# Interleaved two-layer memory attention with gated FFNs: one head grouping for all steps, weight pieces to match, kept tokens of fill blocks, one pool of FFN weight tiles, and a new stored order

## The chip, the cores and the metric

The kernel runs on one core of a Trainium2 chip. The metric is the device time of one execution in microseconds (us); the median of three runs of the kernel before is 1747.63 us. The engines are named as in the profile: PE (matrix products; PEld is its weight load, which overlaps), DVE, ACT and POOL (element work; POOL also issues transfers), and SP, which only issues transfers. Each engine works through its own instructions in the order in which they were issued, and waits for another engine or a transfer only through semaphores.

## The reference, cut to what matters

The input x has 2048 tokens of width D = 512. Two layers are computed, each a recurrent attention and then a gated feed-forward network (FFN), both with a LayerNorm ahead of them and a residual around them; both layers use the same weights.

```python
for s in range(64):                       # 64 segments of 32 tokens, one after another
    h = concat([mem, x[32*s : 32*s+32]])  # 8 memory tokens + 32 tokens = 40
    q, k, v = h @ Wq, h @ Wk, h @ Wv      # 32 heads of 128
    p = softmax(mask(q @ k.T * scale))    # 40 x 40 for each head
    o = sum over heads of (p @ v) @ Wo    # 40 x 512
    mem, out[s] = o[:8], o[8:]            # memory for the next segment
x = x + out;  x = x + (sigmoid(n(x) @ w_gate) * (n(x) @ w_up)) @ w_down   # F = 1792, n: LayerNorm
```

The memory makes the 64 segments of a layer a chain: the Q and K of a segment need the output of the one before.

## The kernel before

**Steps.** The program has 70 steps (`NSTEPS`, L384). Layer 2 follows layer 1 by six segments (`lag`), so steps 6 to 63 treat a segment of each layer together, with 2 x 40 = 80 columns, and steps 0 to 5 and 64 to 69 one segment of one layer, with 40 columns. In steps 0 to 5 the Q and K product carries 14 more columns of layer 2's later segment (54 in all), which are kept in `kx`/`xq` and fetched in steps 6 to 11 (66 columns then).

**One step** (`emit_step`, L771). The heads come in groups. For each group: Q and K by weight tiles of 128x128 (L868), a copy to `qku` by ACT, scores (L904), mask and softmax on DVE and ACT into `pb`, transposes of the probabilities on PE (L950), copies of the transposed blocks into `ptsb` on ACT or DVE (the "spread", L952 to L962: the first as it is, the further ones scaled by a column of zeros and ones, so that the blocks form a block-diagonal matrix), the product with V (L976), a copy to `otsb`, and the sum over heads with `Wo` (L995), whose end releases the next step.

**Head units.** Several heads are stacked on the partitions, one below another, 40 rows each, so that one product with V treats them together; such a stack is a unit. Two-layer steps use `self.sets[3]`: 11 units of three heads (the last of two), taken two units, that is six heads, at a time (6 groups, `self.groups[3]`). One-layer steps use `self.sets[2]`: 16 units of two heads, three units (six heads) at a time, also 6 groups (the last one unit). The probabilities lie in a tile of 66 or 80 columns for each unit, so a one-layer step has 16 transposes of 66 columns and 16 products with V of 2 x 40 = 80 columns.

**V.** V of the tokens is computed ahead, in blocks of four segments (`v_pass` L621ff with matmuls at L635, `v_half` at L673), copied to a staging tile, stored to DRAM (`scr`), and read into the step's `vsb` tile, laid out as the units need; the V of the memory and of the next few tokens comes in the step itself from a strip (matmuls at L762, staging tile `sst`). Because the two groupings lay V out differently in the same tile, `vlast` keeps the last readers of the other layout (L810, L841).

**Start.** `load_weights` (L506) puts the 16.8 MB of attention weights on SP's queue (the loading line is L511): `wv` in 8 pieces of four heads, with x blocks between; then `wq` and `wk` in pieces of 3 + 3, 7 + 7 and 6 + 6 heads, and `wo` in 12 pieces. PE meanwhile computes V of many blocks. The FFN weights (L1089, L1090, L1114) are loaded anew for each of the 32 FFNs, 256 KB at a time, by POOL's queue, into three rings of three tiles (`wg`, `wu`, `wd`); the same nine tiles are staging space for V during the start (`bootp`).

**LayerNorm.** `layernorm_T` normalises 128 tokens and transposes them with four PE products of 128 columns (L595). `pre1` (L735) does it for each block of layer 1. Five blocks (6, 9, 12, 14, 15) are treated twice: once early in `v_fill` (L745), through `ln_x` (L727), which fills free columns of V products with some of their tokens, and later in `pre1`.

**Order.** The program is first listed as tasks with their dependences; a stored permutation (`SEQUENCE`) gives the order of all of them and the choice of engine where a task may go to ACT or DVE, or to the queue of SP or POOL. `replay` (L268) then gives out the places in the pools, and `warm` (L332) picks places where dummy products of a constant tile `hot` (L1214, "fillers" below, 128 to 512 columns each) go ahead of a PE task.

Of the kernel before, what the change touches and what calls it, by code (L numbers as in the profile page):

```python
# [12 lines left out]
BF16 = mybir.dt.bfloat16  # L13
F32 = mybir.dt.float32
# [39 lines left out]
;BKuib6o%lfB&)8j78VFm3*TORJaEeTpTegcj@45cPG=tDu9Cop`gL7BsLuS#OcT}UGbOE%Rvw4_#4%#$D8H!O&97}fvKE=gc~;{D3dThKHFPlwO_o2ZQj%uAntT#b%`=yVSW>zYu00~2SQlskfdun`!ZJ6nE#G~2&?9uc>M  # L54
LJNnK-{6`f<-+4RJ5CZd)}8nOvSmvfKo;s^%eOTt@Z&QQEIDAOJ$@LXy<?hJ}y#Zz34w>^3(tr#O*O)I|-p(v0&hCE6Z=I!u---baa4+5Qm3gUS*53l_a{9Qz2=DO#NG?#SMBs;mj8X%L0%-jPDBKdp!x5<|&*NtR7P%o}ua
+-XmYACJ&^@_Q*%Pqd)VfD(Os7%#QMrvJwasc?e7tW4e|DX`7=(P4&9b1jfW|}nyY`GtB?m|%9YiB{%_E6Z!fQiku2zXKR#fd!bVX{cdYYw6Oa38sdpui0&m(%kDO5RoywpWe0S&Odat#pJd*Y7&%qi}11M_2zTDH){}yQ57
CfOg{V(1Y$JmfqyIFwi1i0YD(h(Op*uWQ$hJP;Bf$yQikUbL75}K_CCXhEehY;YAKq*!3Uc%Xg9$$6Whfxhc_;!XnaeXsWETb0$)eOXEs9v^~2GKd~)jxtdFb@D02?xh_1fp?KW&fTj7T(bbip<45F%z<Q6F`V0&|>^`^b?P
qJ8zT^ZMn>Wcly5FU_gC4bg<ct_t?VIQ91i<1%2up=CHX$olDJee`BwTFh$S(4b<7J|(ro=5g4z*Oc`7TsdGat-Gu458Br)V!dZ#th}Vr^2k08taR4-icZnRx1)Jh)>hE~oGsr}+TM9h@FLc<(r!wd_Q)l$@#>Gc$q3H~Iu8
B@vGI?!$xWWOMXWIIV?oY_(Nj>~oPrOXhF>kb>ie>V?Z|=S{vC&%nc&mvj8fqJ`ng-1GxzLO~&l^?UGKdDeu&>V<rn<D;V-Yi3I0U}(d~*VL}SKef_{vihFam*0lE<Q@4Z?!Z?qE-e`<gdP%rljFd}%1N*?wM}ezvJGP{k@D
$cH#i)?<HymwHhj3y7oDOxbMj(>d6(b!Q+d{(|M_LSlswhN@?|yLvdUV@!>Nk$<yx}-KsEGBSCDfS=C0>x5r{0(p(QEni`j5ECChA3J3+en0nRK&Hcp0NU*(n0!X;LFq2XQO*by|ReBHqg1wB7#*M>TgpbMjBrkTU*99uz+V  # L60
k!4**({(MLwZLEUo#F;deCBV;>LUumfbyI^#!VVbWP5k$-hsK6I{?fV507ZWSJA|AKq%5F`{1CT0QO{)ll|TX=i|DlMvH>_RLPExPwr>G%@9qVJCKh;rJ^&U%*#K4T$Bg>MQlaj#5~$wQ1)H`pM<6emLUsv5wZa)l=){WY>u
1(PrWo8E^2D1I#8XB}8^Ls58~C54o1mj9OA=J+4cPJ+C~sE6k-4&k&ae8X@1F*PsyyFKxb}E<#az2vB}bAQfMX9~5e*e$-cp^b9f#?03PK`_`n347*v6d*kvVd(fEI<GLWdxm4xgBjG)zHL<A%hHEU$OjEB|ok8=Cu$=eft9
7_JwIX$h#wrX%4N>63C6uPVrKBqwjc=Vd@Wy~8jdNx%!(V^~Ph9_85K>}$3*W3jY72M%q-H4DV^R-6iEOJ<_onUb;)O1COU`_I=L_mgyEsJnxeRz8#POUxE1#+`%tEHD44RMPKPW^6eLOcg$o|&zDQ*Nlh>iGK+Ghz|0@nBH
3@kJ$7L<PbAV5AQh4``a`I0#dHH`LBDjM_gK0Pokn)8B2ttp<26cW=A>zgZ=GO3UYclYMQ4dn2>GShncV~(3@lyHdJ{Jxa}Ev3bHmy8Ju@Y9U5ZOE{tO3BJ?jMkiXS|(HfS}kpQC!uhJ!P;9O?}a}e4k*3%iLJX}sgs?w*f=
XgOYGH+cDIV@@a$5ATCuWU#jzExY(5)4aL591Nl?Cx*&6;_u8b|t1>vv?9?^2O-VCaBfCOdyxTq$9dd#ckGW`ET=Jsl6ax*&>JZ_FFIw!m8X)CrH>W%g(JF;g<^At9hhyT|Qp?Z|jy+Uer{4w&$jkIBgR53c-sRQow3V#L`(
$vOBv=vhmUZm13`YMUteDoxBd1P0m9LI(WM5`uXI&1aAxTFXju&Ji(eQ^U~REWO_?68u>zskkLyO|6tP<C+xDQOlw7+iIh5@LT8^X=f)(22(!Me;J5V!ELHErSKTQXZXR{g{GJy12S<ZzfCN&_f+>u8DO|Jvk>@w@&Hj344s
I|6$C3w)^Rgo%Th{vHyA@A7o%+MiYqR?NYb*Y5Cl7XF4+4jP*A>w1`7uq!uTw4y()O)#;`oa-qa=opjk&K5e9gSYBSz3O@(Ud9tbkDP4Tt_3rrXNO|B`^d17v$?eRRhHbXfZ&b=Hgm#DK{Z*>#!yD*yWgOC2CYqRvybr9GP>
# [300 lines left out]
class Kern:  # L368
    def __init__(self, ctx, tc, x_in, mem0, Wq, Wk, Wv, Wo, w_gate, w_up, w_down, out, lag=6, ring=8):
# [17 lines left out]
        self.HH = H // 2  # L387
# [906 lines left out]
```

## Time and profile before

| what | value |
|---|---|
| three runs | 1746.31, 1747.63, 1748.25 us |
| profiled execution, span from first to last instruction | 1747.1 us |
| PE busy | 1733.4 us, 39162 matmuls |
| PEld, DVE, ACT, POOL busy | 85%, 71%, 65%, 49% of the span |
| data moved | 273.41 MB, 156 GB/s on average |
| instructions | 91842 |

The profile gives no time of the profiled execution apart from its span; the median of the runs is 0.5 us above that span. A line of the profile names the engine, the line of the program, the operation, its output and inputs, how many there were, the busy time and the mean duration in ns, and at its end the idle time ahead of them with what ended it. Matmuls overlap: the mean duration of one is not the spacing from one to the next, which is what a row of several products shows by its start and the next row's start.

### The profile page before, as it was taken

What the parts mean: (1) busy time and instruction counts of PE and PEld (TensorE: products, weight loads), DVE (VectorE), ACT (ScalarE), POOL (GpSimd) and SP (SyncE); (2) the same over time, 40 slices, a digit from 0 to 9 for tenths busy, and PEclk for the clock granted to TensorE, in tenths of its full rate; (3) what the DMA queues carried; (4) which work ended last, traced back from release to release, by engine and by line L of the source; (5) the groups of instructions that cost most, each with busy time, mean ns of one, the idle gap of its engine ahead of it and who ended that gap; (6) DMA issues with size and microseconds to landing.
All of it is one profiled execution on the core that took longest, in us unless ns stands there. A gap on an engine that the chain in (4) does not pass through costs nothing.

```text
span 1747.1 us, 91842 instructions
## 1 busy us (share of the span) xinstructions
PE 1733.4 (99%) x39162; PEld 1491.8 (85%) x39162; DVE 1248.4 (71%) x4208; ACT 1128.5 (65%) x3119; POOL 859.0 (49%) x1367
## 2 busy tenths in 40 slices
PE   9999999999999999999999999999999999999998
PEld 4688789889898988989888888989888888988886
DVE  5677777677767776786777767776777776767676
ACT  3576777566666766666666666666665666666564
POOL 5624345635544554445445554544455364454543
PEclk9999999999999999999999999999999999999999
DMA  8935355645645555545555464545455464554644
GB/s 285 320 100 155 109 151 161 195 113 153 174 130 163 156 159 143 165 125 164 152 148 158 136 184 128 166 138 153 132 174 166 139 174 128 144 156 131 178 120 134
DMA packets 145583, 273.41 MB, mean 156 GB/s; under 512 B 39686, under 2 KB 86018, under 8 KB 145174
## 3 DMA queue, kind: packets, MB, share of 16 engines
q0 software_dynamic: 72944, 198.79, 39.8%
q1 hardware_dynamic: 72230, 68.75, 13.3%
q8 instruction: 307, 5.03, 1.2%
q14 instruction: 102, 0.84, 0.2%
HBM read 221.78 MB, written 27.07 MB: 142 GB/s over the span
## 4 chain that ended last, share of the span: by engine, by line
PE 94%; DMA 3%; DVE 1%; SPq 1%; issue 1%; POOL 0%; ACT 0%; POOLq 0%; ACTq 0%
PE bank L868 34%; PE bank L995 17%; PE bank L1097 12%; PE bank L762 8%; PE bank L635 6%; PE bank L1120 6%; PE bank L904 4%; PE bank L976 4%; PE bank L950 2%; PE bank L595 1%; PE bank L1214 1%; DMA wk_sb<-in_A_Wk_dram 1%; DMA wo_sb<-in_A_Wo_dram 0%; PE bank L1065 0%; DMA scr<-wu 0%
## 5 line engine op out<-in xcount | busy, mean ns | idle before, releaser
L868 PE MATMUL bank<-hT,wq_sb 128*128 128x80 bf16 (+3 forms) x8960 | 616.4, 198 | 1.0 <-DVE hT L1008 0.3
L868 PE MATMUL bank<-hT,wk_sb 128*128 128x80 bf16 (+3 forms) x8960 | 616.3, 198 | 0.8 <-DMA wk_sb<-in_A_Wk_dram 0.6
L1228 ACT CAST qku<-bank 128x480 bf16<-128x480 f32 (+4 forms) x770 | 384.7, 508 | 223.7 <-PE bank L868 194.6
L868 PEld LDWEIGHTS <-wq_sb 128*128 128x128 bf16 x8960 | 454.2, 99 | 32.1 <-issue 15.1
L868 PEld LDWEIGHTS <-wk_sb 128*128 128x128 bf16 x8960 | 446.9, 99 | 1.1 <-DMA wk_sb<-in_A_Wk_dram 0.7
L995 PE MATMUL bank<-otsb,wo_sb 128*128 128x80 bf16 (+1 forms) x8960 | 360.2, 198 | 2.2 <-DMA wo_sb<-in_A_Wo_dram 1.3
L918 DVE TENSOR_TENSOR st<-bank,cst 40x240 f32<-40x240 f32 (+3 forms) x768 | 280.5, 368 | 113.2 <-PE bank L904 97.5
L995 PEld LDWEIGHTS <-wo_sb 128*128 128x128 bf16 x8960 | 336.6, 99 | 15.5 <-DMA wo_sb<-in_A_Wo_dram 2.0
L1228 ACT CAST otsb<-bank 128x480 bf16<-128x480 f32 (+3 forms) x420 | 200.2, 483 | 83.4 <-PE bank L976 52.8
L1090 POOL DMA_DIRECT2D wu<-in_B_w_up_dram x217 | 166.5, 768 | 170.0 <-PE bank L950 36.4
L1114 POOL DMA_DIRECT2D wd<-in_B_w_down_dram x217 | 156.9, 723 | 182.0 <-PE bank L1120 39.6
L1224 POOL DMA_DIRECT2D vsb<-sst x351 | 178.2, 512 | 129.6 <-ACT sst L1228 64.7
L1089 POOL DMA_DIRECT2D wg<-in_B_w_gate_dram x217 | 166.4, 767 | 138.1 <-PE bank L1097 56.7
L928 ACT ACTIVATE st<-st 80x240 f32<-80x240 f32 (+3 forms) x420 | 159.2, 381 | 58.0 <-DVE st L925 54.8
L1097 PE MATMUL bank<-xnT,wg 128*128 128x128 bf16 (+2 forms) x1784 | 171.5, 218 | 0.0
L1097 PE MATMUL bank<-xnT,wu 128*128 128x128 bf16 (+2 forms) x1784 | 171.1, 218 | 0.0
L930 DVE TENSOR_REDUCE small<-st 80x6 f32<-80x240 f32 (+3 forms) x420 | 151.5, 363 | 23.4 <-ACT st L928 20.2
L1220 ACT ACTIVATE ptsb<-bank,small 120x160 bf16<-120x160 bf16 (+3 forms) x430 | 156.6, 386 | 17.2 <-PE bank L950 10.7
L904 PE MATMUL bank<-qku 128*128 128x80 bf16 (+1 forms) x2240 | 162.7, 197 | 1.0 <-issue 0.9
L925 DVE TENSOR_TENSOR st<-st,small 80x240 f32<-80x240 f32 (+3 forms) x420 | 155.0, 370 | 5.7
L939 DVE TENSOR_TENSOR pb<-st,small 80x240 bf16<-80x240 f32 (+3 forms) x420 | 154.1, 370 | 5.7
L923 DVE TENSOR_REDUCE small<-st 80x6 f32<-80x240 f32 (+3 forms) x420 | 152.5, 364 | 6.2
(108 smaller groups left out, 2554.1 us busy)
## 6 DMA issues: line engine op xcount, KB each, us to landing
wg<-in_B_w_gate_dram POOLq DMA_DIRECT2D x220, 256.0 KB, 4.2
wu<-in_B_w_up_dram POOLq DMA_DIRECT2D x220, 256.0 KB, 4.2
wd<-in_B_w_down_dram POOLq DMA_DIRECT2D x220, 256.0 KB, 3.9
vsb<-scr SPq DMA_DIRECT2D x137, 66.0 KB
scr<-vst SPq DMA_DIRECT2D x90, 96.0 KB
vsb<-scr POOLq DMA_DIRECT2D x93, 66.0 KB, 3.4
vsb<-sst SPq DMA_DIRECT2D x179, 32.0 KB
vsb<-sst POOLq DMA_DIRECT2D x169, 32.0 KB, 2.8
```

What stands on the lines that cost most here:

```text
L868: nc.tensor.matmul(o_ap, lhsT=W[:, c, h * P:(h + 1) * P], rhs=mv(c), start=(c == 0), stop=(c == DC - 1))
L904: nc.tensor.matmul(s_all(SB)[:, w0 + i, :], lhsT=fview(qku[:, i, 0, 0:1], [(1, P)]), rhs=qku[:, i, 1, 0:ncol], start=True, stop=True)
L918: pl.add("DVE", dve_ns(n, True), lambda gsz=gsz, hs=hs, st=st, SB=SB, pj_=pj_, npj_=npj_, mk=mk, idx=idx: nc.vector.tensor_tensor(out=st[p ...
L928: pl.add("ACT", act_ns(n), lambda hs=hs, st=st: nc.scalar.activation(out=st[pr, hs], in_=st[pr, hs], func=ACTF.Exp, scale=self.scale), r=s ...
L995: nc.tensor.matmul(WB[:, c * ncol:(c + 1) * ncol], lhsT=self.wo[:, h, c * P:(c + 1) * P], rhs=otsb[:, hl, 0:ncol], start=(h == 0 and c == ...
L1089: pl.add("POOL", 760, lambda wg=wg, fs=fs: nc.gpsimd.dma_start(out=wg[:], in_=self.wgv[:, :, fs]), r=[("wo", self.H - 1)], w=[gk] + bt, la ...
L1090: pl.add("POOL", 760, lambda wu=wu, fs=fs: nc.gpsimd.dma_start(out=wu[:], in_=self.wuv[:, :, fs]), r=[("wo", self.H - 1)], w=[uk] + bt, la ...
L1097: nc.tensor.matmul(gu[:, 2 * i + k, 0:n], lhsT=W[:, c, i * P:(i + 1) * P], rhs=xnT[:, c, rw], start=(c == 0), stop=(c == DC - 1))
L1114: pl.add("POOL", 760, lambda wd=wd, ip=ip: nc.gpsimd.dma_start(out=wd[:], in_=self.wdv[:, 2 * ip:2 * ip + 2, :]), w=[dk] + (["boot"] if se ...
L1220: nc.scalar.activation(out=dst, in_=src, func=ACTF.Copy, scale=by)
L1224: {"SP": nc.sync, "POOL": nc.gpsimd}[tk.on].dma_start(out=got[1], in_=got[2])
L1228: nc.scalar.copy(out=dst, in_=src)
```

## The change

- One grouping, `self.rows` and `self.groups`, serves all steps: three heads per unit and two units per group in the one-layer steps too. The V loads of these steps are cut to match (3 instead of 6 from `scr`; 6 instead of 4 from the strip), and `vlast` is gone, since there is one layout.
- The weight pieces follow the units: `wq`, `wk` and `wo` in three rounds, of 3 pieces of three heads, 3 pieces of five, and one piece of eight.
- In `ln_x`, the transposed normalised tokens of the five fill blocks are copied to a staging tile and stored to DRAM (`xt`); `pre1` reads them back (`kept_x`) in place of a second LayerNorm.
- The three rings become one pool of nine tiles (`wtp`), from which each FFN weight and the staging of the start take a tile; a helper `weight` issues the loads.
- The bank pool loses its limits for two kinds of tasks (`{"bg": 3, "v": 3}`), which `replay` only asserts.
- A new stored permutation is used (not shown).

```diff
-        self.sets = {2: [list(range(self.HH)), list(range(self.HH, H))],
-                     3: [list(range(8 * i, 8 * i + 8)) + list(range(24 + 3 * i, min(27 + 3 * i, H))) for i in range(3)]}
+        self.rows = [list(range(8 * i, 8 * i + 8)) + list(range(24 + 3 * i, min(27 + 3 * i, H))) for i in range(3)]
...
+        self.groups = []
+        for u in range(0, self.NU, 2):
+            us = list(range(u, min(u + 2, self.NU)))
+            self.groups.append(([r[k] for k in us for r in self.rows if k < len(r)], us))
...
+        self.xt = dr.tile([self.NBLK * P, D], BF16, name="xt")
...
-        self.wg = [c.tile([P, DC, 2 * P], BF16, name=f"wg{i}") for i in range(self.NG)]
-        self.wu = [c.tile([P, DC, 2 * P], BF16, name=f"wu{i}") for i in range(self.NG)]
-        self.wd = [c.tile([P, 2, D], BF16, name=f"wd{i}") for i in range(self.ND)]
+        self.wt = [c.tile([P, 1024], BF16, name=f"wt{i}") for i in range(9)]
...
-        parts = {0: 3, 3: 6, 9: 7}
-        for heads, us in self.groups[2]:
-            n = len(us)
+        for us in (range(0, 3), range(3, 8), range(8, 11)):
+            hs = [(8 * i + us[0], len(us)) for i in range(3)] if us[0] < 8 else [(24, 8)]
             for nm, sb, v in (("wq", self.wq, wq_v), ("wk", self.wk, wk_v)):
-                for h0 in (us[0], self.HH + us[0]):
-                    m = parts.get(us[0])
-                    if m:
-                        cs = slice(h0 * P, (h0 + m) * P)
-                        ld(sb[:, :, cs], v[:, :, cs], P * self.DC * m * P * 2, [(nm, h) for h in range(h0, h0 + m)])
-            for h0 in (us[0], self.HH + us[0]):
+                for h0, n in hs:
+                    cs = slice(h0 * P, (h0 + n) * P)
+                    ld(sb[:, :, cs], v[:, :, cs], P * self.DC * n * P * 2, [(nm, h) for h in range(h0, h0 + n)])
+            for h0, n in hs:
                 ld(self.wo[:, h0:h0 + n, :], wo_v[:, h0:h0 + n, :], P * n * self.D * 2, [("wo", h) for h in range(h0, h0 + n)])
...
+        pst, B = self.layernorm_T(xb[:, :], key)
+        nc, pl, D = self.nc, self.pl, self.D
+        tt = pl.buf(self.vstp)
+        pl.add(("ACT", "DVE"), copy_ns(D, True), lambda: (tt[:, 0:D].rearrange("p (c n) -> p c n", c=self.DC), pst()), r=[B], w=[tt])
+        pl.add(("SP", "POOL"), {"SP": 430, "POOL": 590}, lambda: ("dma", self.xt[b * P:(b + 1) * P, :], tt[:, 0:D]), r=[tt], w=[("xt", b)], lat=3000.0, nb=P * D * 2)
+        self.kept.add(b)
+        return pst, B
+
+    def kept_x(self, b):
+
+        nc, pl, D = self.nc, self.pl, self.D
+        tt = pl.buf(self.xnp)
+        pl.add("SP", 430, lambda: nc.sync.dma_start(out=tt[:, :], in_=self.xt[b * P:(b + 1) * P, :]), r=[("xt", b)], w=[tt], lat=3500.0, nb=P * D * 2)
+        return (lambda: tt[:, :].rearrange("p (c n) -> p c n", c=self.DC)), tt
...
-        pst, B = self.layernorm_T(xb[:], ("xs", i))
+        pst, B = self.kept_x(b) if b in self.kept else self.layernorm_T(xb[:], ("xs", i))
...
-        ni = 3 if both else 2
-        rows, groups = self.sets[ni], self.groups[ni]
+        rows, groups = self.rows, self.groups
...
-            return vt[r, j, c:c + m] if both else fview(vt[r, 0, 0:1], [(1, 2 * self.NU * P)])[:, c:c + m]
+            return vt[r, j, c:c + m]
...
-            if not both:
-                pcs = [(L * i, h0 - r[0] + o // P, hh) for i, r in enumerate(rows) for h0 in (r[0], r[8]) for o, _, hh in self.runs(h0, 8)]
...
-            hu, hi_ = (1, nu) if ni == 2 else (3, 1)
+            hu, hi_ = 3, 1
...
+                wg, wu = gk, uk = pl.buf(self.wtp), pl.buf(self.wtp)
+                for wt, nm in ((wg, "wg"), (wu, "wu")):
+                    self.weight(wt, nm, jp, [wt], [("wo", self.H - 1)])
...
+                wd = dk = pl.buf(self.wtp)
+                self.weight(wd, "wd", ip, [wd], [("wo", self.H - 1)])
```

More of the change, by code (lines that the diff above doesn't have):

```diff
@@ L145 @@
+qzI#W6;{xHslkB&LfZf
 """
@@ L467, in setup_tiles @@
         self.sstp = Pool(self.sst)
-        self.bootp = Pool([fview(w[:, 0, 0:1], [(1, 1024)]) for w in self.wd + self.wg + self.wu])
+        self.wtp = Pool(self.wt)
         self.xnp = Pool(self.xn)
```

269 lines of the change are left out of this document (118 added, 151 removed).

## The prediction, made before the changed kernel had run

> **What bounds the kernel now.** I read the page first: busy shares, the 40 slices, and the chain of work that ended last.
>
> ```profile
> PE 1733.4 (99%) x39162; PEld 1491.8 (85%) x39162; DVE 1248.4 (71%) x4208; ACT 1128.5 (65%) x3119; POOL 859.0 (49%) x1367
> ...
> PE   9999999999999999999999999999999999999998
> ...
> PE 94%; DMA 3%; DVE 1%; SPq 1%; issue 1%; POOL 0%; ACT 0%; POOLq 0%; ACTq 0%
> ```
>
> PE is busy 99% of the span and is 94% of the chain; the others have slack. So an edit is worth what it takes from PE's instruction stream, or from PE's waits. To see where waits are, I asked for busy times by stretch: up to the first V product (10.23 us), to the end of step 0, of step 5, of step 63, of step 68, and the rest.
>
> ```profile
> 0.00:10.23 10.23, 9.17 (x36) 3.72 (x37) 4.22 (x13) 1.76 (x2) 3.65 (x19) 1.00 0.70 214
> 10.23:79.65 69.42, 64.97 (x783) 36.02 (x783) 41.27 (x121) 32.55 (x87) 42.59 (x85) 1.00 0.96 325
> 79.65:167.10 87.45, 87.21 (x2581) 74.67 (x2580) 65.91 (x235) 65.32 (x243) 36.30 (x58) 1.00 0.49 139
> 167.10:1618.90 1451.80, 1450.10 (x32305) 1273.82 (x32306) 1048.53 (x3533) 956.75 (x2546) 718.58 (x1120) 1.00 0.53 150
> 1618.90:1710.60 91.70, 90.59 (x2708) 79.58 (x2705) 67.28 (x239) 57.83 (x192) 45.30 (x68) 1.00 0.53 152
> 1710.60:1747.10 36.50, 31.36 (x756) 23.96 (x754) 21.23 (x70) 14.25 (x49) 12.57 (x18) 1.00 0.44 126
> ```
>
> Columns: stretch, length, then busy us of PE, PEld, DVE, ACT, POOL, then granted clock, DMA share, GB/s. In one-layer steps (rows 3 and 5) and two-layer steps (row 4) PE lacks 0.2, 1.1 and 1.7 us: bound by PE's stream. The second row differs: PE lacks 4.45 us while DMA is at 96% and 325 GB/s. There the landing of the weights sets the end, as the end of step 0 shows on PE's timeline (a bracket is the idle time ahead and what ended it):
>
> ```profile
> 77.49 0.47 PE L995 MATMUL bank<-otsb,wo_sb 128*128 128x40 bf16 x12 [0.49 <-DMA wo_sb<-in_A_Wo_dram]
> 78.58 0.84 PE L995 MATMUL bank<-otsb,wo_sb 128*128 128x40 bf16 x20 [0.62 <-DMA wo_sb<-in_A_Wo_dram]
> 79.26 0.48 PE L1214 MATMUL bank<-hot 128*128 128x512 bf16 x2
> 79.70 0.26 PE L868 MATMUL bank<-hT,wq_sb 128*128 128x54 bf16 x4
> ```
>
> The last `wo` piece releases the last 20 products; then comes step 1. From 79.70 on, PE runs solid.
>
> **Prices.** Durations of single matmuls overlap, so I take spacings, start to start, from the timeline of a one-layer step and, for wider products, from two pieces of the chain.
>
> ```profile
> 106.29 0.25 PE L950 MATMUL bank<-cst,pb 66*128 66x66 bf16 x3
> 106.38 0.23 PE L904 MATMUL bank<-qku 128*128 128x40 bf16 x3
> ...
> 107.87 0.38 PE L976 MATMUL bank<-ptsb,vsb 80*128 80x80 bf16 x6
> 108.08 1.03 PE L635 MATMUL bank<-wv_sb,xvf 128*128 128x512 bf16 x4
> ```
> ```profile
> 118.05 1.81 PE bank L868 x72
> 520.71 1.79 PE bank L1097 x32
> ```
>
> 66 columns: (106.38 - 106.29)/3 = 30 ns; 80 columns: 0.21/6 = 35 ns; 54 columns: 1.81/72 = 25 ns; 128 columns: 1.79/32 = 56 ns; 512 columns: four from 105.35 to 106.21, 215 ns.
>
> **The change, part by part.** I compared the built instruction lists of both programs, engine by engine, in order.
>
> *Three heads per unit.* A one-layer step has 11 instead of 16 transposes: 192 of 66 columns become 132, -60 x 30 ns = **-1.8 us**, on PE. The products with V go from 16 of 80 columns to 10 of 120 and one of 80 in each step; the columns barely differ: 120 columns take 52 ns (a row of four at L976 in a two-layer step starts at 301.12, the next at 301.33), so 16 x 35 = 560 ns become 10 x 52 + 35 = 555 ns: **-0.1 us** in 12 steps. The price is on ACT and DVE: five groups in each of 12 steps have three spreads instead of two (60 more).
>
> ```profile
> L1220 ACT ACTIVATE ptsb<-bank,small 80x120 bf16<-80x120 bf16 x24 | 8.6, 358 | 1.5 <-PE bank L950 1.1 <-DVE ptsb L1230 0.3
> L1228 ACT COPY ptsb<-bank 40x120 bf16<-40x120 bf16 x21 | 5.1, 248 | 0.1
> ```
>
> Before: 248 + 358 = 606 ns. After, by the rows of two-layer steps (80 columns: 218 plain, 324 scaled): 218 + 2 x 324 = 866 ns, +0.26 us per group, 30 groups x 0.26 x 2 = 15.6 us of ACT or DVE time, of which both have a quarter free in those stretches (65.32 and 65.91 of 87.45 busy). What hides it: between a group's transposes and its V product lie other groups' Q, K and V products, at least 0.6 us of them in both programs, so two spreads on one engine do not quite fit and some V products may wait. Bounds: 0 (all hidden) to +3 us (a fifth of the 15.6 uncovered); I take **+0.5**, close to the hidden end, since PE lacks only 0.24 us in steps 1 to 5 with these spreads in the same place. The loads to `vsb` (3 instead of 6, 6 instead of 4) are on SP and POOL, half idle; nothing.
>
> *Kept tokens.* Five LayerNorms with four transposes each go: -20 x 56 ns = **-1.1 us** on PE. Their DVE and POOL work was off the path (71% and 49%). Added: five copies of 512 columns (0.6 us on ACT), five stores and five loads of 128 KB, on queues with DMA at 53%; their readers are tokens of a block that starts four segments later: nothing. If the load were late, the step's Q and K would wait; I see nothing queued so tightly.
>
> *One pool of weight tiles.* The same 256 KB loads, with any free tile instead of the next of a ring. PE's work between a load's issue and its use, summed by the prices above over the built order, is at least 5.9 us after, 6.5 before (one case 4.8), against landings of 4.2, 4.2 and 3.9 us on the page. Nothing, with a rival below.
>
> *Weight pieces and the start.* Ahead of the last `wo` piece, SP carries 20.24 MB instead of 20.01: 0.23 MB / 325 GB/s = **+0.7 us**, if landing still ends step 0. Fillers: 28 ahead of the first V product become 20 (512 columns mostly, 5.9 to 4.1 us), and between it and the end of step 0, none become 22 (4.4 us at 0.2 each). The latter stand where weights are awaited; if they are, they are free. Q and K can start after nine heads instead of six: 3 x 2 x 0.131 MB = 0.79 MB, +2.4 us, made good if the end is the last `wo` anyway. Bounds for the start: -4 (V 1.8 us sooner, and a 2.1 us wait for `wv` near 20 us closed) to +6.8 (4.4 + 2.4); taken: +0.7, since the row of `wo` at 78.58 is nearest.
>
> *Order.* Between the last `wo` products of a step and the first Q of the next, steps 0 to 2 had nothing; now step 0 has 0.86 us of other work to cover the copy of the memory (the wait at 79.3, filled by two fillers, 0.44 us): **-0.4**. In the two-layer steps the covers (medians) are the same: 0.
>
> Sum: 1747.1 - 1.8 - 0.1 + 0.5 - 1.1 + 0.7 - 0.4 = 1744.9 us of span; +0.5 to the median of the runs (1747.63 - 1747.1): **1745.4 us**.
>
> The granted clock is 1.00 in every stretch, and no idle time in the trace exceeds 2.1 us. The Trainium skill ("TensorE: Matmul & The Clock Gate", "Part 1: The HAM clock gate") says that about 3.4 us of idleness halve the clock, and some 3.4 us of work restore it; no run shown here reaches that. By that rule a start that waited longer, unfilled, would lose another 1.7 us (3.4 us of work at half rate), an estimate from that page; it speaks for the new fillers. The same page ("Back-to-back issue gap") gives about 81 ns for each 128-column product in a stream of weight loads and products; by it the 20 LayerNorm transposes would be worth 1.6 us and the time 1744.9. The trace has 56 ns, and decides.
>
> **Rivals.**
> A, the forecast: PE's stream shrinks by 3 us, the start ends with the last `wo`. 1745.4, by the bounds of the spread 1743 to 1748.
> B: the start shortens. First V products 1.8 us sooner, and the wait for `wv` closed: 1745.4 - 0.7 - 1.8 - 2.1 = 1740.8. For it: PE has idle time there. Against: DMA is at 96%, so PE sooner does not end sooner.
> C, slower: step 0 waits for nine heads of `wq` and `wk`, and fillers run where nothing is missing: 1745.4 - 0.7 + 2.4 + 4.4 = 1751.5. It decides when the fillers stand after the landing of what they precede. Against: the same bytes end the step.
> D, slower: loads of FFN weights with 0.6 us less lead make PE wait 0.2 us in each of 32 FFNs: +6.4, 1751.8. It decides when landings exceed 5.9 us; the row has 4.2.
> E: the 66-column and LayerNorm work removed was itself a cover, and waits take its place: 1747.6, no change.
>
> **How the numbers follow.** Chances: A 0.46, B 0.30, C 0.10, D 0.07, E 0.07. What a measurement can tell from no change is 0.2%, 3.5 us: faster is below 1744.1, slower above 1751.1. Of A, 0.10 lies below 1744.1. Faster: 0.30 + 0.10 = 0.40; same: 0.36 + 0.07 and 0.01 of C = 0.44; slower 0.16. The range reaches to B's 1740.8 with 1 us below, and to the edge of C and D: 1739.8 to 1751.6.
>
> **What would show it.** Right: 132 transposes of 66 columns at the same spacing, 300 LayerNorm transposes, PE in the one-layer steps still within 0.5 us of full, the end of step 0 ended by `wo`, a granted clock of 1.00. Wrong: a bracket on the V product (L976's successor) naming ACT or DVE; PE waits on `wg`, `wu`, `wd`; a first Q product with a long `wk` wait; or two-layer steps whose stretch differs by over 2 us, which nothing above foresees.

## The result, and the profile after

The changed kernel takes **1759.91 us** (median of 6 runs, 1757.88 to 1763.96) beside 1747.94 us of the kernel before on the same chip (6 runs, 1746.16 to 1754.47): ratio 1.0065, 95% interval 1.0049 to 1.0082. It is slower by 12 us where 2 us less were predicted, and outside the range. The profiled execution has a span of 1757.3 us, 10.2 us more than the one of before.

The page of the changed kernel, the lines that answer to the first fence of the prediction:

```profile
PE 1724.7 (98%) x38832; PEld 1490.2 (85%) x39035; DVE 1258.4 (72%) x4149; ACT 1153.6 (66%) x3223; POOL 867.0 (49%) x1390
...
PE   8899999999999999999999999999999999999998
...
PE 89%; DVE 4%; DMA 3%; issue 2%; ACT 1%; POOL 0%; SPq 0%; DVEq 0%; POOLq 0%; ACTq 0%
```

PE was busy for less (1724.7 for 1733.4 us; 203 of its 39035 products, PEld's count, have no record) in a longer span, its first two slices are at 8, and its share of the chain fell from 94% to 89%. The same busy times by stretch (up to the first V product, end of step 0, of step 5, of step 63, of step 68, and the rest):

```profile
0.00:8.00 8.00, 6.39 (x28) 2.58 (x29) 4.71 (x17) 2.14 (x3) 5.54 (x26) 1.00 0.66 203
8.00:85.99 77.99, 69.05 (x791) 37.94 (x800) 40.08 (x113) 36.56 (x102) 42.62 (x81) 1.00 0.95 311
85.99:174.45 88.46, 87.45 (x2521) 74.41 (x2528) 67.23 (x240) 67.28 (x260) 36.48 (x58) 1.00 0.51 141
174.45:1629.61 1455.16, 1440.21 (x32107) 1272.87 (x32283) 1057.35 (x3477) 971.03 (x2587) 724.84 (x1139) 1.00 0.53 151
1629.61:1721.87 92.26, 91.10 (x2652) 79.18 (x2660) 69.17 (x238) 61.21 (x216) 45.95 (x70) 1.00 0.50 141
1721.87:1757.30 35.43, 30.52 (x741) 23.22 (x739) 19.83 (x68) 15.37 (x55) 11.57 (x17) 1.00 0.38 114
```

"Busy" hides most of what happened: a matmul of some 200 ns that starts every 25 ns leaves no hole in the sum of busy times when a start is late. So I counted the matmuls of both programs and gave each its spacing, by the prediction's rows (columns x 0.417 ns + 2.3 ns, at least 25 ns: 25, 30, 35, 56, 216 ns for 54, 66, 80, 128, 512 columns). Length less work less fillers is PE's idle time. In us:

| stretch | length before, after | work | fillers | idle |
|---|---|---|---|---|
| to the end of step 0 | 79.45, 85.99 | 62.52, 62.58 | 5.88, 8.47 | 11.06, 14.94 |
| steps 1 to 5 | 87.47, 88.47 | 82.90, 81.87 | 0.97, 1.08 | 3.60, 5.50 |
| steps 6 to 63 | 1451.80, 1455.16 | 1418.32, 1417.63 | 2.92, 2.43 | 30.57, 35.09 |
| steps 64 to 68 | 91.70, 92.26 | 87.20, 86.39 | 0.32, 0.97 | 4.18, 4.89 |
| the rest | 36.72, 35.42 | 27.89, 27.30 | 1.08, 0.54 | 7.74, 7.58 |

Two things blur the first rows. The end of step 0 is set 0.2 us behind the start of its last `wo` product before, and 0.5 us behind it after; from last `wo` product to last `wo` product the start is 6.2 us longer and steps 1 to 5 are 1.4 us longer. And the first fillers start 427 ns apart instead of 216, up to 6.5 us before and 3.8 us after (the trace's record of the clock begins there, so the first stretch reads 1.00): 2.7 and 1.2 us of the idle in the first row are this slow running.

The work is 3.0 us less, as predicted. The start takes 6.5 us more, the two-layer steps 3.4 us, and the one-layer steps 1.6 us more instead of 1.8 us less. Profiles of one kernel differ by some us in the start, so I also use the kernels of this study that leave a stretch alone: the start took 76.6 to 80.5 us in seven profiles with the start of before (some with other spreads in step 0) and 84.1 to 86.0 in three with the changed one (90.3 in a fourth, a_dve, whose clock was halved for 6.8 us); steps 6 to 63 took 1451.5 to 1454.3 in eight profiles in the order of before and 1455.2 to 1457.1 in seven in the changed order (1456.7 and 1458.9 in two more, whose clock was halved for 3.4 us there). Both gaps are real; in steps 1 to 5 (87.5 to 89.3, and 88.5 to 90.6) the ranges overlap.

PE's timeline at the end of step 0 of the changed kernel, which answers to the prediction's fence from that place:

```profile
73.20 1.08 PE L1198 MATMUL bank<-hot 128*128 128x512 bf16 x5
76.46 0.47 PE L963 MATMUL bank<-ptsb,vsb 120*128 120x120 bf16 x6 [2.17 <-DMA vsb<-sst]
...
84.08 1.57 PE L981 MATMUL bank<-otsb,wo_sb 128*128 128x40 bf16 x56
85.71 0.81 PE L620 MATMUL bank<-wv_sb,xvf 128*128 128x512 bf16 x3
86.36 0.27 PE L855 MATMUL bank<-hT,wq_sb 128*128 128x54 bf16 x4
```

No `wo` product (L981) waits any more. The first V product of step 0 does (L963), after five fillers; it starts at 76.46 us, where before it started at 67.58. What PE waited for in the whole execution, largest first (us in total, times, longest):

```profile
PE bank L620 <- DMA wv_sb<-in_A_Wv_dram: 3.7, 3, 1.5
PE bank L963 <- DMA vsb<-scr: 3.0, 2, 1.9
PE bank L963 <- DMA vsb<-sst: 2.2, 1, 2.2
PE bank L855 <- DMA wk_sb<-in_A_Wk_dram: 1.4, 1, 1.4
```

The loads of V into `vsb` are new in this list, and nothing waits for the FFN weights in `wt`: rival D did not come. Where the V loads stand in SP's queue explains the first of them. Before (SP's timeline: two of the V loads, then the last `wo` pieces; three of the other loads from `scr` for step 0 go between 41 and 51 us and a small one at 60 us, on SP's and POOL's queues):

```profile
46.29 2.58 SPq L1224 DMA_DIRECT2D vsb<-scr  x1
49.33 1.78 SPq L1224 DMA_DIRECT2D vsb<-scr  x1
...
60.20 0.45 SPq L511 DMA_DIRECT2D wo_sb<-in_A_Wo_dram  x1
62.03 0.63 SPq L1224 DMA_DIRECT2D scr<-wu  x1
62.71 9.38 SPq L511 DMA_DIRECT2D wo_sb<-in_A_Wo_dram  x10
```

After, the same queue:

```profile
60.11 4.25 SPq L499 DMA_DIRECT2D wo_sb<-in_A_Wo_dram  x3
64.40 1.84 SPq L1208 DMA_DIRECT2D vsb<-scr  x1
66.29 0.70 SPq L499 DMA_DIRECT2D wo_sb<-in_A_Wo_dram  x1
67.42 0.89 SPq L1208 DMA_DIRECT2D vsb<-scr  x2
68.36 0.40 SPq L499 DMA_DIRECT2D wo_sb<-in_A_Wo_dram  x1
68.87 0.93 SPq L1208 DMA_DIRECT2D vsb<-sst  x1
```

The program ties them together: a V load of step 0 may go only after the `wo` piece that holds the last head (`+ ([("wo", self.H - 1)] if t == 0 else [])`, in both kernels). Before, that head lay in a small piece of its own, issued at 34.3 us; now it lies in the one piece of eight heads, issued at 60.1 us. The last V load, from the strip (`sst`), is not tied itself but stands behind the others in SP's queue; it takes 7.35 us to land, under a DMA share of 95%, and the chain of waits goes through it: `68.87 7.35 DMA vsb<-sst`.

### The profile page after: what moved, and what is told of

Same layout as the page of the kernel before. It is cut to its first block, busy times and chain, and to the rows that moved or that the text cites. A ratio compares the mean times of both kernels' runs of the same rounds, so it can differ in the third digit from the quotient of the medians.

```text
span 1757.3 us, 91441 instructions
## 1 busy us (share of the span) xinstructions
PE 1724.7 (98%) x38832; PEld 1490.2 (85%) x39035; DVE 1258.4 (72%) x4149; ACT 1153.6 (66%) x3223; POOL 867.0 (49%) x1390
## 4 chain that ended last, share of the span: by engine, by line
PE 89%; DVE 4%; DMA 3%; issue 2%; ACT 1%; POOL 0%; SPq 0%; DVEq 0%; POOLq 0%; ACTq 0%
PE bank L855 31%; PE bank L981 17%; PE bank L1083 10%; PE bank L759 7%; PE bank L620 7%; PE bank L1104 4%; PE bank L963 4%; PE bank L891 4%; PE bank L937 2%; DMA wv_sb<-in_A_Wv_dram 1%; DVE st L905 1%; PE bank L580 1%; DMA vsb<-scr 1%; DMA xs<-in_A_x_dram 1%; DVE small L910 0%
## 5 line engine op out<-in xcount | busy, mean ns | idle before, releaser
L1212 ACT CAST qku<-bank 128x480 bf16<-128x480 f32 (+3 forms) x770 | 382.0, 506 | 210.6 <-PE bank L855 179.6
L855 PEld LDWEIGHTS <-wq_sb 128*128 128x128 bf16 x8960 | 453.0, 99 | 25.4 <-issue 12.7
L981 PE MATMUL bank<-otsb,wo_sb 128*128 128x80 bf16 (+1 forms) x8960 | 356.0, 198 | 0.7 <-issue 0.5
L981 PEld LDWEIGHTS <-wo_sb 128*128 128x128 bf16 x8960 | 334.0, 99 | 11.6 <-issue 0.8
L1208 POOL DMA_DIRECT2D vsb<-sst x365 | 184.7, 510 | 193.0 <-ACT sst L1212 55.6
L1083 PE MATMUL bank<-xnT,wt 128*128 128x128 bf16 (+2 forms) x3568 | 242.4, 218 | 0.5
L1014 POOL DMA_DIRECT2D wt<-in_B_w_up_dram x220 | 168.3, 765 | 128.6 <-PE bank L981 25.8
L1014 POOL DMA_DIRECT2D wt<-in_B_w_gate_dram x220 | 168.4, 766 | 117.9 <-PE bank L937 37.9
L1014 POOL DMA_DIRECT2D wt<-in_B_w_down_dram x220 | 159.0, 723 | 116.7 <-PE bank L1083 28.5
L1083 PEld LDWEIGHTS <-wt 128*128 128x128 bf16 x3568 | 205.4, 98 | 4.0 <-issue 0.2
L1204 ACT ACTIVATE ptsb<-bank,small 120x160 bf16<-120x160 bf16 (+3 forms) x517 | 181.4, 375 | 18.7 <-PE bank L937 15.7
L1208 POOL DMA_DIRECT2D vsb<-scr x190 | 100.6, 531 | 166.0 <-PE bank L937 48.0
L917 DVE TENSOR_REDUCE small<-st 80x6 f32<-80x240 f32 (+3 forms) x420 | 152.0, 363 | 23.3 <-ACT st L915 19.6
```

The costliest lines, as they stand in the source:

```text
L855: nc.tensor.matmul(o_ap, lhsT=W[:, c, h * P:(h + 1) * P], rhs=mv(c), start=(c == 0), stop=(c == DC - 1))
L981: nc.tensor.matmul(WB[:, c * ncol:(c + 1) * ncol], lhsT=self.wo[:, h, c * P:(c + 1) * P], rhs=otsb[:, hl, 0:ncol], start=(h == 0 and c == ...
L1014: self.pl.add("POOL", 760, lambda: nc.gpsimd.dma_start(out=wt[:, 0:1024].rearrange("p (c f) -> p c f", c=n), in_=src), w=keys, lat=4700.0, ...
L1083: nc.tensor.matmul(gu[:, 2 * i + k, 0:n], lhsT=W[:, (2 * c + i) * P:(2 * c + i + 1) * P], rhs=xnT[:, c, rw], start=(c == 0), stop=(c == DC ...
L1204: nc.scalar.activation(out=dst, in_=src, func=ACTF.Copy, scale=by)
L1208: {"SP": nc.sync, "POOL": nc.gpsimd}[tk.on].dma_start(out=got[1], in_=got[2])
```

## The experiments

All ratios are to the kernel before on the same chip (medians 1747.6 to 1750.0 us there), with the 95% interval. Those with a_ start from the changed kernel, those with b_ from the one before; adding or dropping a line shifts some line numbers by one to three. "Start" is the time to the end of step 0.

### The start

**b_late: the kernel before, with the V loads late.** Only the order of the queues changes.

```diff
-vsb<-scr x6 (step 0), ..., wo pieces
+wo pieces, vsb<-scr x6 (step 0)
```

> The kernel before with one thing moved: the six loads of the tokens' V of step 0 stand on SP's queue behind the wo pieces issued up to 72 us, instead of at 42 to 60 us. Theory (late V loads make the long start): first V product of step 0 goes from 67.6 to 78 us or later, end of step 0 from 79.5 to 86 to 89 us, time 6 to 9 us longer. Rival (the landing of the weights ends step 0 anyway): end of step 0 and time within 1 us of before.

Measured: 1759.27 us, ratio 1.0059 (1.0039 to 1.0079); start 85.93 us, first V product at 74.13:

```profile
PE bank L975 <- DMA vsb<-scr: 7.5, 1, 7.5
```

The one wait, put into the kernel before, gives the start of the changed kernel (85.93 beside 85.99 us) and most of its loss. But PE's clock fell in it, as the granted clock (third column from the right) shows for three stretches of 10 us:

```profile
60.00:70.00 10.00, 5.63 (x96) 3.53 (x97) 5.41 (x18) 3.29 (x11) 0.00 (x0) 1.00 0.93 301
70.00:80.00 10.00, 5.65 (x56) 3.44 (x58) 2.42 (x10) 3.56 (x11) 2.30 (x5) 0.66 0.64 197
80.00:90.00 10.00, 9.94 (x275) 8.08 (x278) 4.36 (x15) 5.84 (x23) 8.42 (x17) 1.00 0.57 154
```

**b_late_f: the same with 28 fillers of 512 columns ahead of the first V product**, to tell the clock from the wait.

```diff
-            fill = {i: (..., n) for i, n in {118: 91, ..., 13893: 14}.items()}
+            fill = {i: (..., n) for i, n in {118: 91, ..., 13893: 14, 431: 112}.items()}
```

> The kernel before with the V loads of step 0 behind wo, as in the earlier run (end of step 0 at 85.9 beside 79.5, clock 0.50 and 0.68 in the 8 us after the wait of 7.5 us), and 28 fillers of 512 columns (6 us) ahead of the first V product. If the clock took part: from the two slices some 2.3 us are won, end of step 0 at 83.5, and 4 us stay as the price of late V loads. Rival (after the wait PE waits for wo anyway, so its clock costs nothing): end of step 0 at 85.5 to 86.

Measured: 1755.83 us, ratio 1.0039 (1.0024 to 1.0054); clock 1.00 in the start (halved once later, for 3.4 us at 1662 us), first V product at 75.35 after a wait of 2.01 us behind the fillers, start 85.22. The clock was worth 0.7 us of the start, not 2.3, so the rival's reading is the nearer one. The late V loads alone hold: some 6 us.

**a_nofill: the changed kernel without the 22 fillers of step 0.**

```diff
-            fill = self.pl.warm(order)
+            fill = {i: (..., n) for i, n in {115: 65, 118: 11, 728: 6, ...}.items()}
```

(Cut. The places and lengths of the changed kernel's fillers are written out, without four: 369, 430, 451 and 478.)

> The changed kernel without its 22 fillers between the first V product and the end of step 0 (4.4 us of PE); nothing else moves. Theory (the start is late because the V of step 0 arrives late, the fillers stand in waits): end of step 0 stays at 86.0 us within 0.5, the idle time ahead of the first V product of step 0 grows by what the fillers took, time unchanged. Rival (the fillers themselves cost): end of step 0 at about 81.6 us, time 4.4 us shorter.

Measured: 1763.19 us, ratio 1.0081 (1.0064 to 1.0098); start 88.08, fillers 4.10 us for 8.47, idle 21.40 for 14.94. Idle time took their place, and the start grew by 2.1 us instead of staying: rival C's fillers "where nothing is missing" are not there. Without them the clock fell twice, to 0.67 in the 4 us from 56 and to 0.68 in those from 80, which the idle above includes.

**a_gate: V loads of step 0 ahead of wo in the changed kernel** (issued from 48.5 us; one strip load goes to POOL), without those fillers.

```diff
-wo pieces, vsb<-scr x3, vsb<-sst
+vsb<-scr x3, vsb<-sst, wo pieces
...
-                            r=[...] + ([("wo", self.H - 1)] if t == 0 else []),
+                            r=[...],
```

> The changed kernel, the same fillers left out, and the three loads of the tokens' V of step 0 no longer wait for the wo piece that holds the last head: they are issued ahead of the wo pieces, and the one strip load that stood behind them goes to POOL's queue. PE's order is kept. Theory (these loads set the start): the first V product of step 0 goes from 76.5 to about 72 us, the end of step 0 from 86.0 to 82 to 83.5, time 3 to 4 us below the kernel without fillers. Rival (the last wo pieces, issued at 73.6 to 74.6, set the end): V product earlier, end of step 0 at 85.5 or later, time the same.

Measured: 1763.04 us, ratio 1.0073 (1.0053 to 1.0094); first V product at 79.10, start 88.36. The wait for V in step 0, 2.3 us in a_nofill, is gone, but others stand in the start: `wv` 4.5 (4.3 in a_nofill), `wk` 3.9 (1.7), `wq` 1.5 (1.0) us. My theory, that undoing this wait undoes the loss, fell. The clock was below 1.00 in several places (0.66 from 56 to 60 us, 0.62 from 68 to 72), so it was run again with fillers.

**a_gate_f: the same with all fillers kept.**

> The changed kernel with the loads of the tokens' V for step 0 ahead of wo on the queues, as in the earlier run of that kind, but with all fillers kept, so that the clock stays at 1.00. Theory (the first V product waits for its V loads, and in the earlier run a clock of 0.62 to 0.95 hid the gain): end of step 0 at 82 to 84 beside 86.0, the whole 2 to 4 us faster than the changed kernel, 1756 to 1758. Rival (weights are what is late in this start: wk, wq, wv): end of step 0 at 85.5 or later, the whole at 1760.

Measured: 1765.92 us, ratio 1.0096 (1.0081 to 1.0111); first V product at 76.47 without a wait, start 86.74. The clock was 1.00 from 27 us on; from 23.3 to 26.7 us it was halved, which cost PE 1.6 us well ahead of a wait of 2.66 us for `wk`. So the clock did not hide the gain that was expected; the rival holds. PE's timeline and SP's queue show what is late instead:

```profile
66.06 0.28 PE L855 MATMUL bank<-hT,wk_sb 128*128 128x54 bf16 x4 [2.66 <-DMA wk_sb<-in_A_Wk_dram]
```
```profile
45.81 3.08 SPq L1208 DMA_DIRECT2D vsb<-scr  x3
54.00 0.59 SPq L499 DMA_DIRECT2D wq_sb<-in_A_Wq_dram  x1
55.94 0.49 SPq L499 DMA_DIRECT2D wk_sb<-in_A_Wk_dram  x1
```

In the changed kernel the last piece of `wq` goes at 48.39 and that of `wk` at 54.94. Behind the V loads they go 5.6 and 1.0 us later: SP issues one transfer between 48.9 and 53.3 us (the profile puts its waits there down to landings of `wk` and `wq` pieces and of stores of V), and from 50 to 60 us the queues move 238 GB/s instead of 337.

**a_wv: wv pieces ahead of the x blocks**, as in the kernel before, where the first is issued at 0.81 us; in the changed one it goes at 2.68, behind four x blocks.

```diff
-x block x4, wv piece 0, wv piece 1
+wv piece 0, x block x2, wv piece 1, x block x3
```

> The changed kernel with the first piece of wv at the head of SP's queue and the second one ahead of the third x block, instead of behind four x blocks; everything else, fillers too, as in the changed kernel. Theory (V loads of step 0 set the start): waits for wv fall from 3.7 to about 2 us, the first V product of step 0 still waits until 75 to 76.5 us, time the same within 1 us. Rival (the late wv sets the start): end of step 0 and time 2 us earlier.

Measured: 1760.96 us, ratio 1.0068 (1.0049 to 1.0087). The start went to 83.85, 2.1 us better (the rival's figure; no wait for `wv` is left, and V is awaited for 1.7 us), but steps 6 to 11 lost 3.65 us: a V product waits for 2.8 us at 289 us, and the clock is 0.57 in the 4 us after it.

**a_gate_wv: both moves**, without the fillers.

> The changed kernel without the 22 fillers, with step 0's V loads ahead of the wo pieces and with the first two wv pieces early, both edits together. Theory (late V loads and late wv both lengthen the start, each hidden behind the other when it is mended alone): end of step 0 from 86.0 to 82 us or earlier. Rival (pieces of wq and wk for nine heads end the waits of the start): end of step 0 at 84 us or later, with waits for wq and wk of over 3 us.

Measured: 1762.36 us, ratio 1.0083 (1.0064 to 1.0101), start 87.21, first V product at 74.73. The end is as late as the rival has it, but not for its reason: the wait for `wk` is 0.9 us and none for `wq` is listed; `wo` is awaited for 1.9 us, and the clock was halved three times for 3.4 us.

**a_gate_wv_f: both moves with all fillers.**

> Both moves (V loads of step 0 ahead of wo, the first wv pieces ahead of the x blocks) with all fillers kept. Theory: both waits go, end of step 0 at 80 to 82, the whole at 1754 to 1756. Rival (the queues carry the same bytes, so what is moved ahead delays wq and wk): end of step 0 at 84 or later, with waits on wq, wk or wo of 3 us or more together.

Measured: 1764.14 us, ratio 1.0093 (1.0069 to 1.0116); start 85.86, clock 1.00 in it, first V product at 75.46. Rival again: 2.6 us of waits for `wk`, 0.7 for `wo`, and 2.4 at one LayerNorm transpose.

### The one-layer steps

**b_spread3: the kernel before, each scaled spread of the one-layer steps issued three times** (PE's stream unchanged).

```diff
-                    return (dst, pt[:, :, 0:nj, :]) + ((self.lower[i][r], "scaled") if i else ())
+                    return (dst, pt[:, :, 0:nj, :]) + ((self.lower[i][r], 1 if both else 3) if i else ())
...
-                        nc.scalar.activation(out=dst, in_=src, func=ACTF.Copy, scale=by)
+                        [nc.scalar.activation(out=dst, in_=src, func=ACTF.Copy, scale=by) for _ in range(times)]
```

> The kernel before with each scaled spread of the one-layer steps issued three times over, the same values each time: 144 more spreads of about 0.3 us on ACT and DVE, more than twice what the change adds; PE's stream and order are as before. Theory (the third spread is what the one-layer steps of the changed kernel lost): steps 1 to 5 and 64 to 68 together grow by 5 us or more. Rival (other work hides it, the loss is from the order): they grow by less than 2 us.

Measured: 1788.02 us, ratio 1.0222 (1.0207 to 1.0238); steps 1 to 5 took 106.17 us for 87.47, steps 64 to 68 108.15 for 91.70. The waits of PE, largest first:

```profile
PE bank L976 <- ACT ptsb L1228: 9.8, 16, 1.3
PE bank L976 <- ACT ptsb L1220: 7.4, 15, 0.9
```

The products with V wait for ACT's spreads. With spreads this long, these steps are not bound by PE's stream alone. (The clock averaged 0.96 in its steps 1 to 5, worth up to 4 us, and 1.00 in steps 64 to 68.)

**b_spread2: the same, issued twice** (0.36 us more for each group).

> The kernel before with each scaled spread of the one-layer steps issued twice (0.36 us more for each group; three times gave 18.7 us in steps 1 to 5 and 16.4 in 64 to 68 for 0.72 us). With a slack of 0.23 us for each group: 0.13 us x 60 groups, 8 us, steps 1 to 5 at 91.5. In proportion, without slack: half of the three-fold run, 17.5 us, steps 1 to 5 at 97. The change adds 0.26 us for each group: 2 us by the first, 12 us by the second.

Measured: 1761.24 us, ratio 1.0069 (1.0054 to 1.0084); steps 1 to 5 94.81, steps 64 to 68 97.08: 12.7 us more than in the profile of before, between the two expectations. The first 0.36 us costs 0.21 us for each of the 60 groups, the next 0.36 us 0.37 us (22.4/60): a slack of some 0.15 us, and then one for one (steps 64 to 68 alone, at a clock of 1.00: 0.18 and 0.37 us). By that the change's 0.26 us, in five of the six groups of these ten steps, would cost 0.11 us x 50 = 5.5 us in an order not made for it, an estimate from these two runs.

**b_dve and a_dve: a second spread given to DVE**, wherever all spreads of a one-layer group were on ACT (48 and 47 groups). Only the stored choice of engine changes.

```diff
-spread i=1 of the group: ACT
+spread i=1 of the group: DVE
```

> The kernel before; in the one-layer steps, wherever both spreads of a group run on ACT (48 of the groups), the scaled one goes to DVE, beside the plain one. It takes about 0.3 us off the time from transposes to the product with V, the opposite of issuing the spread three times. Theory (some 0.23 us of slack for each group, worked out from the run with three spreads): only the idle that spreads cause goes, at most the 3.6 us of PE's idle in steps 1 to 5: that stretch from 87.5 to 86.5 or 87, steps 64 to 68 from 91.7 to 91.2, the whole 0.5 to 1.5 us faster. Rival (the cost is proportional, no slack): 0.3 us for each of 48 groups as far as idle is there: steps 1 to 5 at 84.5, the whole 5 us faster. Rival 2 (DVE's queue is the later one): slower by 1 us or more.

> The changed kernel; in the one-layer steps, wherever all three spreads of a group run on ACT one after another (47 of the groups), the second one goes to DVE at its place in the order. Theory (ACT's third spread is what the one-layer steps lost: idle time of PE in steps 1 to 5 went from 3.6 to 5.5 us, in 64 to 68 up by 0.7): the spreads of a group end some 0.25 us sooner, idle in steps 1 to 5 falls to about 4, the stretch from 88.5 to 87, steps 64 to 68 from 92.3 to 91.6, together 2 us. Rival (the products with V wait for something else there, or DVE's own queue is as late): both stretches within 0.5 us.

Measured: 1768.04 us, ratio 1.0112 (1.0094 to 1.0130), and 1775.61 us, ratio 1.0157 (1.0138 to 1.0177): 20 and 16 us slower than without it. Both theories fell; of the rivals only "slower by 1 us or more" has the sign. In b_dve, steps 1 to 5 (after the bar: idle time ahead, and what ended it):

```profile
L1222 DVE TENSOR_SCALAR ptsb<-bank,small 80x120 bf16<-80x120 bf16 x22 | 5.9, 270 | 6.0 <-ACT ptsb L1228 3.9 <-PE bank L950 2.1
L1228 ACT COPY ptsb<-bank 40x120 bf16<-40x120 bf16 x21 | 5.3, 251 | 6.8 <-DVE ptsb L1222 5.9 <-PE bank L950 0.5
```

The two spreads do not run side by side: each waits for the other one's engine; in the program both write the same `ptsb` tile. While the engine waits, what stands behind it waits as well: PE's largest wait in b_dve is 5.3 us in all, at the transposes, for DVE's `pb`.

**a_pure and b_pure: groups already split between the two engines made whole** (14 in the changed order, 9 in that of before).

```diff
-spreads of the group: ACT and DVE
+spreads of the group: one engine
```

> The changed kernel; the 14 groups of the one-layer steps whose spreads are split between ACT and DVE get all their spreads on one of the two. If split groups cost there what they cost in the runs that split 48 groups (0.43 us each): steps 1 to 5 from 88.5 to 86 or 86.5, 64 to 68 from 92.3 to 90, the whole 4 to 6 us faster than the changed kernel. If the groups that are split stand where the handover is hidden: within 1 us in both stretches.

> The kernel before with its 9 split groups of the one-layer steps made whole on ACT. If each costs 0.43 us: up to 3.9 us faster, the whole at 1745 beside 1749, steps 64 to 68 from 91.7 to 90. If they stand where it is hidden: the same within 1 us.

Measured: 1761.65 us, ratio 1.0078 (1.0060 to 1.0097), steps 1 to 5 89.65, 64 to 68 93.46; and 1749.11 us, ratio 1.0011 (0.9999 to 1.0022). Nothing is won (both stretches of a_pure are 1.2 us longer than in the changed kernel's profile): the orders had split groups where the handover is hidden, and nothing shows these as part of the loss. Nor is b_pure a faster kernel.

### The two-layer steps and the pool

The idle of a two-layer step is the same to 0.1 us from profile to profile, in both orders, except in some steps. Step 10 took 22.9 us in all nine profiles in the order of before and 23.1 to 25.0 in eight in the changed one; step 46 took 28.3, and 28.5 to 30.5 us (last `wo` product to last `wo` product; by spacings the work is the same to 0.3 us). A ninth profile had 27.4 in step 10 and another 32.3 in step 46, each with the clock halved for 3.4 us there. These steps are the first of a block of layer 2, whose V was stored a few us earlier. In the changed kernel one V product of the first group starts, and the next ones wait:

```profile
288.84 0.53 PE L963 MATMUL bank<-ptsb,vsb 120*128 120x120 bf16 x7 [1.92 <-DMA vsb<-scr]
...
1197.14 0.53 PE L963 MATMUL bank<-ptsb,vsb 120*128 120x120 bf16 x7 [1.04 <-DMA vsb<-scr]
```

**a_lead: the changed kernel with 345 tasks moved and 17 engines chosen anew, so that these V loads are issued earlier.**

```diff
-..., stores of V, strip loads, V loads, ...
+..., stores of V, V loads, strip loads, ...
```

> The structure of the changed kernel and its fillers, in another order: 345 of the 14006 tasks are moved and 17 change engine, so that V loads of a step are issued earlier. Theory (the order put the V loads of some steps too late, the structure is not at fault): waits of the V products for vsb in steps 1 to 69, 3.9 us in the changed kernel, fall below 1.5 us, and the time falls by 2 to 4 us. Rival (the structure costs the time): waits move elsewhere, time the same.

Measured: 1766.60 us, ratio 1.0102 (1.0077 to 1.0126), steps 6 to 63 1459.2. V products wait still, at other steps too (2.11 us at 290, 1.77 at 617). The theory that an order with earlier loads mends it was not borne out by this order.

**a_vfree and b_vfree: V loads that follow no fresh store.** The loads of steps 6 to 63 read other V of the same size.

```diff
-                sc_ = self.scr[j][s * XS + lo:s * XS + lo + nx, ...
+                sc_ = self.scr[0 if both else j][(t - (t > LAG) if both else s) * XS + lo:(t - (t > LAG) if both else s) * XS + lo + nx, ...
...
-                            r=[("vd", j, b, q, h) ...
+                            r=[("vd", 0 if both else j, (t - (t > LAG)) // BLK if both else b, q, h) ...
```

> The changed kernel with one thing altered: in steps 6 to 63 each load of the tokens' V reads the V that was stored in DRAM for the segment one step earlier in layer 1, of the same size and at the same place in the queues, so that no load waits for a store made shortly before. What it leaves out: the attention of these steps uses the wrong tokens' V. Theory (the two-layer steps lost 3.4 us because V stored just before is read too late at steps 10, 46 and 58): steps 6 to 63 fall from 1455.2 to 1450 (5.1 us of waits gone), the whole to 1755 beside 1760. Rival 1 (the waits only move to what is queued next, as they did at the start): steps 6 to 63 at 1454 or more. Rival 2 (the loads are late because four FFN weight loads share the queues with them, not because of the store): the gaps at 286, 1196 and 1497 us remain.

> The kernel before with the same one alteration (in steps 6 to 63 the loads of the tokens' V read V stored a step earlier in layer 1, wrong tokens, same sizes and places). Theory (in the order of before these loads are in time): steps 6 to 63 stay at 1451.8 within 0.5 us, the whole at 1748 to 1749. Rival (both orders lose time to these loads, and the changed one only somewhat more): 6 to 63 fall by 2 us or more.

Measured: 1760.63 us, ratio 1.0067 (1.0053 to 1.0082), steps 6 to 63 1455.18; and 1749.22 us, ratio 1.0005 (0.9993 to 1.0016), steps 6 to 63 1454.54. The waits at 286 and 1196 us are gone (step 10 1.5 us shorter, step 46 1.2), but steps 18, 24 and 42 got longer by 0.9, 0.7 and 0.9 us, and in b_vfree step 50 by 2.0. The sum of a_vfree stays: rival 1. That b_vfree grew by 2.7 us in these steps neither of its expectations had. The single steps prove little. Without the alteration, step 10 took 23.1 to 23.7 us in six other profiles of the changed order (23.5 in a_vfree), step 46 took 28.5 in one, as in a_vfree, step 18 was 0.4 to 1.4 us longer than in the changed kernel's profile in six, and step 50 was 1.8 and 1.5 us longer in b_spread3 and b_pure. The gap at 1497 us is still there in a_vfree (0.84 us). So that the fresh store makes these waits is not shown, nor why the changed order has 3 to 4 us more of them.

**b_pool: the kernel before with one pool of nine weight tiles**, in its own order.

```diff
-        self.wg = [c.tile([P, DC, 2 * P], BF16, name=f"wg{i}") for i in range(self.NG)]
...
+        self.wt = [c.tile([P, 1024], BF16, name=f"wt{i}") for i in range(9)]
```

> The kernel before with the one pool of nine FFN weight tiles instead of three rings, in its own order and with its own fillers. My term for the pool is nothing: time within 0.2% of before. Rival (a load that takes any tile waits for a late reader): waits for wt at L1097 or L1120, time 2 us or more longer.

Measured: 1749.50 us, ratio 0.9998 (0.9989 to 1.0008). The pool costs nothing.

## Why the prediction was wrong

- **Where it broke first: "bound by PE's stream".** The prediction read this from busy times ("PE lacks 0.2, 1.1 and 1.7 us"). By spacings PE was idle, or slow at the very start, for 57 us before, 31 us of it in the two-layer steps and 3.6 in steps 1 to 5, and for 68 after. The durations that overlap were seen, and used for the prices only. The Trainium skill says in "Perfetto Trace Analysis", "Identifying the Most-Contended Engine", that the busy share of matmuls is no good measure, since they are pipelined. This case agrees: 99% and 98% busy, with 3% and 4% idle by spacings (57 of 1747 and 68 of 1757 us).
- **The start, +0.7, measured +6.5.** The term rested on "if landing still ends step 0", taken from the wait of the last `wo` product. That product was only what came last; the first V product stood 11 us ahead of it, and in the changed kernel its loads were held by the gate on the last head's `wo` piece. The text counted bytes ahead of the last `wo` piece, but not that a regrouped piece moves what is tied to it: the tied V loads went from 41 to 60 us (five of six by 51) to 64 to 68 us, and one strip load behind them to 69. That late V loads cost 6 us is shown (b_late, b_late_f). That undoing it in the changed kernel gains nothing is shown as well (a_gate_f): there the last `wq` and `wk` pieces come late. So late V loads are enough for this loss, but they are not shown to be all that makes the changed start long. Bounds of -4 to +6.8 did hold it, by luck: the upper one was made of fillers and of the wait for nine heads, and neither was the cause.
- **Rivals at the start.** B had the first V products 1.8 us sooner, and they were, by 2.2 (8.00 for 10.23 us; 1.5 us of it since fewer fillers ran at the slow rate of the first us), but the wait for `wv` grew from 2.7 to 4.9 us (by spacings) instead of closing. C named a longer wait for `wk` and idle fillers; the wait came (1.4 us beside 0.6 before, where C had 2.4 more), the fillers were free (a_nofill).
- **The third spread, +0.5.** The mechanism was named, and the 0.26 us for each group held (216 + 323 + 328 = 867 ns on ACT in the profile after, for 866), but 0.5 us was too small a price for what these steps lost. Steps 1 to 5 and 64 to 68 took 1.56 us more with 1.84 us less work, so 3.4 us came in, 0.8 of it more fillers; the forecast had 0.5 for it. The ground for 0.5 ("PE lacks only 0.24 us in steps 1 to 5") is the same misreading of busy. That spreads stand within some 0.15 us of the path there is shown (b_spread2, b_spread3); that the third spread is all of the 3.4 us is not. The sign that the text named, a wait of a V product for ACT or DVE, is not in the changed kernel's profile: in its steps 1 to 5 the idle ahead of V products is 0.9 us by spacings, for 0.2 before, and the rest of the new idle stands ahead of other products.
- **Two-layer steps, 0, measured +3.4.** The text set them to 0 since "the covers (medians) are the same". A median over 58 steps can't show a wait in a few of them. What makes these waits in the new order stays open.
- **What held.** The work fell by 3.0 us. The pool costs nothing (b_pool), FFN weights are not awaited, and the granted clock of the changed kernel stays at 1.00 from its first record on. The move from step 0 to step 1 is open: the 0.2 us waits there are below what profiles of one kernel differ by.

What stays open: which of several limits that lie within a few us of each other sets the changed start (each one mended brought up the next: V loads, then `wk` and `wq`, and the new order also puts 1.4 us more work and 2.3 us more fillers ahead of the first V product), and what in the new order makes V loads of some two-layer steps late. The kept tokens were not tried alone: without the new order they need another one, whose own effect could not be told from theirs.

## What to carry to other kernels

Judge an engine whose instructions overlap by starts, not by busy time: count the instructions, give each its spacing, and the idle time that is left is what a change can lose or win. When pieces of a load are regrouped, look for everything that is tied to a piece (here a gate on the last head), not only at who reads it. Where several waits are nearly equal, mending one shows the next; price a change in such a stretch by its worst neighbour, not by the wait that happens to end last.

## What the runs showed of the hardware

The clock falls after shorter waits than the prediction allowed. In a_vfree PE waited 1.96 us for V at 72.6 us, after fillers had run to that point, and the granted clock was halved from about 75 to 78.5 us (the clock is the third column from the right):

```profile
74.00:75.00 1.00, 0.47 (x9) 0.51 (x10) 0.10 (x1) 0.00 (x0) 0.00 (x0) 1.00 0.75 190
75.00:76.00 1.00, 0.78 (x7) 0.36 (x4) 0.59 (x4) 0.96 (x5) 0.00 (x0) 0.55 1.03 361
76.00:77.00 1.00, 1.00 (x30) 0.96 (x28) 0.79 (x2) 0.14 (x1) 0.00 (x0) 0.50 0.98 340
77.00:78.00 1.00, 0.91 (x19) 0.86 (x17) 0.00 (x0) 0.36 (x1) 0.00 (x0) 0.50 1.07 367
78.00:79.00 1.00, 0.86 (x4) 0.37 (x4) 0.00 (x0) 0.00 (x0) 0.54 (x1) 0.74 1.08 373
```

In a_gate_f a wait of 2.15 us that ended at 22.3 us was followed by 3.4 us at half the clock (23.3 to 26.7 us), and in a_wv one of 2.81 us that ended at 289.0 us as well (289.2 to 292.6 us). In b_late a wait of 7.5 us halved it for 6.8 us, some 4.4 of them after PE had work again. The changed kernel's own wait of 2.17 us at the same place as in a_vfree left it at 1.00, and so did the one of 2.08 us by spacings in the kernel before (at 25.7 us). The Trainium skill ("TensorE: Matmul & The Clock Gate", "Part 1: The HAM clock gate") has the gate look at windows of about 3.4 us that run freely; falls of 3.4 and 6.8 us, after some waits of 2 us and none after others, fit such windows, but here a wait did not have to fill one for the clock to fall.
